# The second product of a dense layer, from the third unit on, as three passes of float16 halves

## Chip, core and metric

One core of one Trainium2 chip runs the whole program. Its engines are TensorE (PE; its weight loads are listed as PEld), VectorE (DVE), ScalarE (ACT), GpSimd (POOL) and SyncE (SP, which here only issues DMAs). The metric is device time in microseconds (us) of one launch, the median of several runs. Shares and durations come from one profiled execution.

## What is computed

Attention with a top-32 mask, then a dense layer with softplus (the "first expert layer"), then a layer of eight routed experts. All inputs are float32 or wider; the tokens are 4 x 576 = 2304, the width is 512.

```python
def _attn_ref(q, k, v):                       # (4, 8, 576, 64)
    scores = scale * np.matmul(q, k.transpose(0, 1, 3, 2))
    kth = np.partition(scores, -top_k, axis=-1)[..., -top_k:-top_k + 1]
    scores = np.where(scores >= kth, scores, -1000000000.0)
    ...
    return np.matmul(attn, v)

def _moe_ref(x, w_in, w_out):                 # 2304x512, 512x2048, 2048x512
    h = x @ w_in
    g = np.maximum(h, 0.0) + np.log1p(np.exp(-np.abs(h)))
    return g @ w_out

def _moe2_ref(x, w_gate, w1, w2):             # 8 experts, 512x1024 and 1024x512
    expert_idx = np.argmax(x @ w_gate, axis=1)
    ...
    out[mask] = gate_w[mask, None] * (np.maximum(xe @ w1[e], 0.0) @ w2[e])
```

## The kernel before

The program has two parts. **Part one** does attention and the dense layer, **part two** the routed experts.

Attention runs over 72 *score groups*, each of two tiles of 128 query rows by 576 keys. A group's scores are made on PE (L406, in two PSUM tiles `sa` and `sb`), copied by ACT (L416, L452), sorted on DVE by eights (L446 to L472) until the 32nd largest is known, masked and exponentiated by ACT and POOL in turn (ACT L480, POOL L481, ACT L482), split into float16 halves (ACT L490, POOL L491 and L492), transposed by DMA (L494) and multiplied with V on PE three groups later (L509, L511, "attention product").

The dense layer runs over ten *units* (`UNITS`, numbered 1 to 10), which become ready as their attention rows are finished. Units 4 and 10 have one tile of 128 tokens, all others two, so 18 tiles in all. A unit takes 16 *steps*, one for each block of 128 of the 2048 hidden columns. In `layer1` a step has 12 float16 matmuls (L596: the split `w_in` against the split `x`), then ACT does Exp (L610, with a sum that is read out) and Ln (L611) and leaves `g`, the block of 128 hidden columns by 256 tokens. Two steps later (`GLAG`) `layer2` multiplies `g` with the block of `w_out` into the PSUM tile `y`, one product of 128x512 for each tile.

For units 1 to 8 that product is a float32 matmul (L636), which the trace shows as two instructions. Units 9 and 10 (`TAIL = 9`) do it in three passes: `g` and the block of `w_out` are each split into two tiles of type float32r by `halves` (ACT copy L622, DVE subtraction L623), and PE takes high by high, high by low and low by high (L633). The tiles for this are borrowed: `g`'s halves sit in the tiles of the pool `raw` in which q, k and v were loaded, `w_out`'s in the tile `w` of the pool `dec`. The block of `w_out` is split again for each of the two units.

`w_out` itself lies as 16 float32 blocks in `w_out_s`, decoded from the input during the first 24 score groups. After a unit's last step its `y` is copied out (L640) and the side steps of `route` follow, one per step, which choose the expert and scatter rows and places to DRAM (SP L702, POOL L705). `early_slots` plans the first slots of part two the same way.

**What sets the order.** Each engine has one queue, executed in order. The program is emitted with priorities (softmax ahead, dense layer behind), and a scheduler then writes each engine's queue; an instruction with free operands may be put far ahead of where it was emitted. Part two's tiles lie in the memory of part one's pools and have to wait until those are free. In part two, `split` (ACT L898, DVE L899) makes float32r halves of expert weights for the products L937 and L950.

## Time and profile before

| | us |
|---|---|
| median of 3 runs (1062.65 to 1066.71) | 1065.49 |
| the profiled execution | 1060.82 |
| its span, first to last instruction | 1059.1 |
| PE busy (share of the span) | 889.8 (84%) |
| DVE busy | 853.0 (81%) |
| ACT busy | 801.3 (76%) |
| POOL busy | 603.0 (57%) |

In the trace, decoding and the first groups fill the first 146 us; units 1 to 8 run beside attention from 147 us on, the last attention product starts at 721 us, units 8 (its end), 9 and 10 fill the time to 822 us, and part two the rest. No engine bounds the whole span: the shares have to be read by stretch. PE's "busy" includes the latency of pipelined matmuls, so its work is better counted as instructions times the distance from one start to the next.

### The profile page before, as it was taken

How to read it: one execution, taken by the hardware profiler on the slowest of the kernel's cores; microseconds unless marked ns; L12 is line 12 of the kernel's file. 1: busy time of each engine (PE TensorE's matmuls, PEld its weight loads, DVE VectorE, ACT ScalarE, POOL GpSimd, SP SyncE). 2: the span in 40 equal slices, each digit the busy share in tenths (PEclk: the TensorE clock that was granted, in tenths of full speed). 3: DMA queues.
4: the chain of work that ended last, by engine and by line, in shares of the span. 5: the costliest groups of instructions: out<-in, count | busy, mean ns of one | idle time of the engine just before them, and what ended most of it. 6: DMA issues, size and time to landing. Idle time of an engine off the chain costs nothing.

```text
span 1059.1 us, 22197 instructions
## 1 busy us (share of the span) xinstructions
PE 889.8 (84%) x7146; PEld 659.0 (62%) x7146; DVE 853.0 (81%) x3021; ACT 801.3 (76%) x1866; POOL 603.0 (57%) x631
## 2 busy tenths in 40 slices
PE   1124379666989797998999999999999999999994
PEld 0012256344656565665666667666787999999993
DVE  5789999899988688997889999965357987777774
ACT  5889899888799678897998898863677655555553
POOL 3889898998678587776877877762001022111111
PEclk9986579777999989998999999999999999999998
DMA  7897898985889987659876755564301667766760
GB/s 189 202 216 165 201 202 176 200 173 100 129 117 171 124 131 136 108 85 150 156 155 113 116 85 98 80 93 124 112 11 32 164 214 240 246 221 220 234 213 24
DMA packets 295859, 156.97 MB, mean 148 GB/s; under 512 B 257524, under 2 KB 257652, under 8 KB 295732
## 3 DMA queue, kind: packets, MB, share of 16 engines
q1 hardware_dynamic: 292116, 145.73, 65.2%
q0 software_dynamic: 3616, 9.72, 2.6%
q8 instruction: 58, 0.95, 0.4%
q14 instruction: 69, 0.57, 0.2%
HBM read 77.89 MB, written 11.11 MB: 84 GB/s over the span
## 4 chain that ended last, share of the span: by engine, by line
PE 47%; DVE 13%; DMA 9%; ACT 8%; POOL 6%; issue 4%; SPq 1%; POOLq 0%; ACTq 0%; DVEq 0%
PE h L937 10%; PE y L950 9%; PE h L596 9%; PE y L636 8%; DVE mx L472 3%; PE y L633 3%; DVE wk L468 3%; POOL e L481 2%; DMA vn<-in_v_dram 2%; DMA kt<-st 2%; DMA pT<-p 2%; PE m L509 1%; PE sb L406 1%; POOL p L492 1%; ACT e L482 1%
## 5 line engine op out<-in xcount | busy, mean ns | idle before, releaser
L636 PE MATMUL y<-w_out_s,g 128*128 128x512 f32 x480 | 233.7, 610 | 5.3 <-ACT g L611 4.7
L596 PE MATMUL h<-xT,w_in_s 128*128 128x256 f16 (+1 forms) x1920 | 224.5, 267 | 9.1 <-POOL w_in_s L260 3.2
L596 PEld LDWEIGHTS <-w_in_s 128*128 128x128 f16 x1920 | 173.6, 100 | 70.2 <-issue 43.6
L481 POOL TENSOR_TENSOR e<-s,e 128x576 f32<-128x576 f32 x144 | 202.5, 1421 | 16.9 <-ACT e L480 16.5
L472 DVE MAX8 mx<-wk 128x8 f32<-128x128 f32 (+2 forms) x432 | 200.8, 500 | 0.1
L492 POOL TENSOR_TENSOR p<-e,p 128x512 f16<-128x512 f32 x144 | 167.3, 1162 | 0.0
L406 PEld LDWEIGHTS <-q 128*128 128x128 f16 (+1 forms) x640 | 56.1, 109 | 175.5 <-issue 127.6
L468 DVE MATCH_REPLACE8 wk<-mx,wk 128x128 f32<-128x128 f32 (+1 forms) x432 | 144.6, 341 | 0.1
L636 PEld LDWEIGHTS y<-w_out_s,g 128*128 128x128 f32 x480 | 83.7, 195 | 69.0 <-issue 57.6
L917 POOL DMA_INDIRECT out_dram<-ot,idx x19 | 19.5, 1028 | 175.7 <-DVE ot L916 172.9
L482 ACT ACTIVATE e<-e,bias 128x576 f32<-128x576 f32 x144 | 110.5, 768 | 11.0 <-POOL e L481 10.4
L406 PE MATMUL sa<-kt,q 128*128 128x256 f16 (+1 forms) x320 | 53.0, 305 | 77.0 <-DMA kt<-st 22.9
L937 PEld LDWEIGHTS h<-xT,wf 128*128 128x128 f32 x864 | 111.8, 191 | 5.3 <-ACT wf L898 0.2
L937 PE MATMUL h<-xT,wf 128*128 128x256 f32 x864 | 113.9, 283 | 0.0
L950 PE MATMUL y<-wf,hT 128*128 128x512 f32 x432 | 112.8, 398 | 0.0
L406 PE MATMUL sb<-kt,q 128*128 128x320 f16 (+1 forms) x320 | 63.1, 340 | 50.9 <-ACT s L452 50.8
L480 ACT ACTIVATE e<-s,kths 128x576 f32<-128x576 f32 x144 | 105.0, 766 | 0.9
L509 PEld LDWEIGHTS <-pT 128*128 128x128 f16 (+1 forms) x1440 | 88.2, 107 | 24.4 <-issue 18.3
L509 PE MATMUL m<-v,pT 128*128 128x65 f16 (+1 forms) x1440 | 95.2, 202 | 9.5 <-DVE x L536 4.9
L490 ACT ACTIVATE p<-e 128x576 f16<-128x576 f32 x144 | 97.4, 678 | 5.0 <-DMA pT<-p 4.3
L491 POOL TENSOR_TENSOR p<-e,p 128x64 f16<-128x64 f32 x144 | 46.1, 320 | 73.6 <-ACT p L490 72.2
L610 ACT ACTIVATE sa<-h 128x256 f32<-128x256 f32 (+1 forms) x160 | 56.3, 352 | 40.1 <-PE h L596 39.3
(213 smaller groups left out, 1817.1 us busy)
## 6 DMA issues: line engine op xcount, KB each, us to landing
w1r<-in_moe_w_dram SPq DMA_DIRECT2D x20, 1024.0 KB
w2r<-in_moe_w_dram SPq DMA_DIRECT2D x20, 1024.0 KB, 6.6
w<-in_moe_w_in_dram SPq DMA_DIRECT2D x16, 512.0 KB, 4.2
w<-in_moe_w_out_dram SPq DMA_DIRECT2D x16, 512.0 KB
rows<-xr SPq DMA_DIRECT2D x37, 128.2 KB, 2.7
qn<-in_q_dram SPq DMA_DIRECT2D x16, 288.0 KB, 3.6
kn<-in_k_dram SPq DMA_DIRECT2D x16, 288.0 KB, 3.1
vn<-in_v_dram SPq DMA_DIRECT2D x16, 288.0 KB, 4.7
```

Of the source, the lines that this page charges most:

```text
L406: last_qk[0] = nc.tensor.matmul(ps[p0:p1], lhsT=qs[:, h, r0:r1, :].rearrange("p r d -> p (r d)"), rhs=kt[:, k0:k1, cs], start=first, stop= ...
L468: nc.vector.match_replace(out=to, in_to_replace=mx[:, i, 8 * j:8 * j + 8], in_values=src[i], imm_value=NEG)
L472: nc.vector.max(out=mx[:, i, 8 * j + 8:8 * j + 16], in_=src[i])
L480: nc.scalar.activation(e[i], s[i], AF.Relu, bias=kths[:, 2 * gi + i], scale=-K_UP)
L481: nc.gpsimd.tensor_tensor(out=e[i], in0=s[i], in1=e[i], op=ALU.subtract)
L482: nc.scalar.activation(e[i], e[i], AF.Exp, bias=bt[:, i], scale=SCORE)
L492: nc.gpsimd.tensor_tensor(out=p16[:, S + D:], in0=e[i][:, 0:S - D], in1=p16[:, 0:S - D], op=ALU.subtract)
L509: nc.tensor.matmul(o[:, h, 0:D + 1], lhsT=pT(r), rhs=v16[:, h, c, 0:D + 1], start=r == 0, stop=r == R - 1)
L596: nc.tensor.matmul(hps[:, :n], lhsT=w_in_s[:, c, j, p, o:o + 128], rhs=xT[:, 0:len(u.tiles), r, c, :], start=m == 0, stop=m == 3 * KD - 1)
L636: nc.tensor.matmul(u.y[i], lhsT=g[:, cs], rhs=w_out_s[:, f, :], start=f == 0, stop=f == KF - 1)
L937: nc.tensor.matmul(h, lhsT=w1f[:, a, c, :], rhs=xT[:, b, c, :], start=n == 0, stop=n == 3 * KD - 1)
L950: nc.tensor.matmul(y[i], lhsT=hT[g][:, a, i * 128:i * 128 + 128], rhs=w2f[:, b, :], start=g == 0 and n == 0, stop=g == KF2 - 1 and n == 2)
```

## The change

From unit 3 on (`HALF_Y = 3` takes the place of `TAIL`) the product is done in three passes of **float16** halves. `w_out` is turned into halves once, while unit 3 runs, and in place: `w_out_t` has one block more at its front, and the two float16 halves of block f are written over float32 block f-1. `g`'s halves are one float16 tile of the size of the old `g`; Ln now writes into Exp's tile `sa`. The subtraction in `halves` moves from DVE to POOL. A sum of the absolute high halves (`y_sums`, 16 ACT instructions emitted with unit 8) goes into the test at the end. The tile `gt` of the softmax goes; its values are kept in a slice of `wk`. Units 1 and 2 stay as they were.

```diff
-TAIL = 9
+HALF_Y = 3
...
+    y_sums = const.tile([128, KF], F32, name="y_sums")
...
-                          (e_sums, 0.0, E_MAX), (w_sums.rearrange("p a b -> p (a b)"), 64.0, 6.0e4)):
+                          (e_sums, 0.0, E_MAX), (w_sums.rearrange("p a b -> p (a b)"), 64.0, 6.0e4),
+                          (y_sums, 64.0, 6.0e4)):
...
-    w_out_s = wp.tile([128, KF, DM], F32, name="w_out_s")
+    w_out_t = wp.tile([128, KF + 1, DM], F32, name="w_out_s")
+    w_out_s = w_out_t[:, 1:]
...
-            gh = row.tile([128, 2, QS], F32, name="gt", bufs=1)
             w2 = row.tile([128, 2, S], F32, name="wk", bufs=WKB)
+            gh = w2[:, :, QS:PS]
...
-            nc.vector.tensor_tensor(out=w2[:, :, QS:PS], in0=gl, in1=gh, op=ALU.min)
+            nc.vector.tensor_tensor(out=gh, in0=gl, in1=gh, op=ALU.min)
...
-        g = gp.tile([128, 256], F32, name="g")[:, :n]
+        half_y = flags is not None and u.number >= HALF_Y
+        g = a[:, :n] if half_y else gp.tile([128, 256], F32, name="g")[:, :n]
...
-        if u.number >= TAIL:
-
-            g2 = raw.tile([128, R * D], F32R, name="qkv"[f % 3] + "n")[:, :2 * n].rearrange("p (s t) -> p s t", s=2)
-            halves(g2, g)
-            w2 = dec.tile([128, 2 * C], F32R, name="w", bufs=DWB).rearrange("p (s c) -> p s c", s=2)
-            halves(w2, w_out_s[:, f, :])
-            g = g2, w2
+            if u.number >= HALF_Y:
+                if u.number == HALF_Y:
+                    halves(w_half(f), w_out_s[:, f, :])
+                g2 = gp.tile([128, 256], F32, name="g").bitcast(F16).rearrange("p (s t) -> p s t", s=2)[:, :, :n]
+                halves(g2, g)
+                g = g2
+            if u.number == len(UNITS) - 2:
+                t = dec.tile([128, C], F32, name="t")
+                nc.scalar.activation(t, w_half(f)[:, 0], AF.Abs, accum_out=y_sums[:, f:f + 1])
...
+    def w_half(f):
+        return w_out_t[:, f, :].bitcast(F16).rearrange("p (s c) -> p s c", s=2)
...
-        nc.vector.tensor_tensor(out=t[:, 1], in0=src, in1=t[:, 0].bitcast(F32), op=ALU.subtract)
+        nc.gpsimd.tensor_tensor(out=t[:, 1], in0=src, in1=t[:, 0], op=ALU.subtract)
...
-            if u.number >= TAIL:
+            if flags is not None and u.number >= HALF_Y:
                 for m, (a, b) in enumerate(PASSES):
-                    nc.tensor.matmul(u.y[i], lhsT=g[0][:, a, cs], rhs=g[1][:, b, :], start=f == 0 and m == 0,
+                    nc.tensor.matmul(u.y[i], lhsT=g[:, a, cs], rhs=w_half(f)[:, b, :], start=f == 0 and m == 0,
                                      stop=f == KF - 1 and m == 2)
```

The line numbers of the changed kernel are higher by 3 to 9 (L406 becomes L409, L596 L599, L610 L614, L636 L645, L633 L642, L898 L907, L937 L946).

**The queues.** The scheduler writes all of them anew. First ACT, at the 27th score group, while unit 2 runs. `s` are copied scores, `e` and `p` the softmax, `sa`, `g` the dense layer's Exp and Ln, `x2T` and `ex` belong to `route`. Before:

```order
L416 ACTIVATE s<-sa 128x2x256
L610 ACTIVATE sa,e_sums<-h 128x256
L490 ACTIVATE p_3538<-e 128x576
L611 ACTIVATE g<-sa 128x256
L479 ACTIVATE kths<-mx 128x2
L480 ACTIVATE e<-s,kths 128x576 x2
L610 ACTIVATE sa,e_sums<-h 128x256
L452 ACTIVATE s<-sb 128x2x320
L611 ACTIVATE g<-sa 128x256
L458 ACTIVATE bias<-mx 128x2
```

The same place in the changed kernel:

```order
L419 ACTIVATE s<-sa 128x2x256
L615 ACTIVATE g<-sa 128x256
L482 ACTIVATE kths<-mx 128x2
L493 ACTIVATE p_3514<-e 128x576
L631 ACTIVATE w_out_s<-w_out_s 128x512
L675 ACTIVATE x2T<-h 128x512
L483 ACTIVATE e<-s,kths 128x576 x2
L624 ACTIVATE t,y_sums<-w_out_s 128x512
L614 ACTIVATE sa,e_sums<-h 128x256
L455 ACTIVATE s<-sb 128x2x320
L461 ACTIVATE bias<-mx 128x2
L631 ACTIVATE w_out_s<-w_out_s 128x512
```

The copies of `w_out` (L631) and the sums emitted with unit 8 (L624) stand here, between the softmax's instructions, with their subtractions in POOL's queue. Counted over the rows of groups 24 to 31: ACT gets 14 copies of `w_out`, 13 sums, 18 Exp where 14 were and 20 Ln or copies of `g` where 14 were; POOL gets 14 subtractions of `w_out` and 4 of `g`. Groups 53 to 61: ACT 20 copies of `g`, 20 Exp for 17, 19 Ln for 17; POOL 21 subtractions of `g`. Groups 62 to 69: 16 copies and 16 subtractions.

PE, from the last attention product on. Before:

```order
L509 MATMUL m<-v_8275,pT 128x65
L690 MATMUL h<-oh,before 128x8
L691 MATMUL h<-ohcum,ones 128x8
L596 LDWEIGHTS w_in_s
L596 MATMUL h<-xT,w_in_s 128x256
...
L636 MATMUL y<-w_out_s,g 128x512 x4
```

In the changed kernel:

```order
L512 MATMUL m<-v_8493,pT 128x65
L599 LDWEIGHTS w_in_s
L599 MATMUL h<-xT,w_in_s 128x256
...
L642 LDWEIGHTS g
L642 MATMUL y<-w_out_s,g 128x512
```

What moved is the place of the last attention product in PE's queue: of the 1920 matmuls of `layer1`, 1464 stood ahead of it before and 1557 now. Behind it, up to part two's first L950, stood 264 `layer1` matmuls of 256 columns, 192 of 128, 16 float32 products and 144 float32r passes; now 171, 192 and 150 float16 passes. The 60 matmuls of part two's L937 that precede the first L950 stood behind unit 10 and are now strewn over units 9 and 10, since ACT's first `split` stands after step 131 of 160 instead of after all of them.

POOL, after the last softmax instruction. `xh` are halves of the dense layer's input, `si` small constants. Before:

```order
L557 TENSOR_TENSOR xh<-xtail_6877,xh 128x512
L1013 IOTA si 128x12
L1013 IOTA si 128x8
L705 DMA table<-ids,dsti 18688x1
L557 TENSOR_TENSOR xh<-x_10337,xh 128x512
L885 DMA xg_12344<-rows,idx 128x513
L885 DMA xg_12346<-rows,idx 128x513
L885 DMA xg_12379<-rows,idx 128x513
L885 DMA xg_12381<-rows,idx 128x513
L705 DMA table<-ids,dsti 18688x1 x5
```

In the changed kernel:

```order
L632 TENSOR_TENSOR g<-sa,g 128x256 x3
L1022 IOTA si 128x12
L1022 IOTA si 128x8
L894 DMA xg_12753<-rows,idx 128x513
L894 DMA xg_12755<-rows,idx 128x513
L560 TENSOR_TENSOR xh<-x_10684,xh 128x512
L632 TENSOR_TENSOR g<-sa,g 128x256 x6
L894 DMA xg_12788<-rows,idx 128x513
L894 DMA xg_12790<-rows,idx 128x513
L632 TENSOR_TENSOR g<-sa,g 128x256 x9
L714 DMA table<-ids,dsti 18688x1
```

POOL's queue was nearly free of compute there; now a subtraction of each step (L632) stands in it behind gathers and scatters.

## Rows read from the trace of the kernel before

**Rows 1.** Stretches: us, busy of PE, PEld, DVE, ACT, POOL, PEclk, DMA, GB/s.
```profile
100.00:200.00 100.00, 67.25 (x559) 43.18 (x558) 96.64 (x303) 91.04 (x203) 89.84 (x86) 0.76 0.86 189
...
264.00:336.00 72.00, 68.62 (x582) 46.12 (x580) 63.21 (x266) 61.53 (x152) 53.65 (x57) 0.98 0.86 136
336.00:538.00 202.00, 183.56 (x1653) 123.72 (x1652) 168.07 (x698) 166.75 (x420) 147.52 (x157) 0.94 0.80 131
538.00:613.00 75.00, 74.15 (x647) 51.11 (x647) 71.69 (x297) 66.75 (x163) 58.97 (x64) 1.00 0.69 116
613.00:678.00 65.00, 64.67 (x590) 44.24 (x587) 63.65 (x265) 57.59 (x136) 49.21 (x53) 1.00 0.58 91
...
722.00:830.00 108.00, 106.47 (x785) 82.86 (x783) 63.30 (x261) 71.82 (x214) 9.90 (x10) 1.00 0.24 69
```

**Rows 2.** First and last start of L509, then of L950, by line.
```profile
L509 PE MATMUL m<-v,pT x1440: 190/193/263, 61.7 to 721.0; 128*128 128x65 f16 x143, 128*64 128x65 f16 x37
...
L950 PE MATMUL y<-wf,hT x432: 387/393/486, 830.4 to 1034.9; 128*128 128x512 f32 x144
```

**Rows 3.** Chain that ended last, in order of time: start, us, what.
```profile
743.10 1.31 PE h L596 x12
744.41 1.72 PE y L636 x4
...
758.98 1.40 PE y L633 x6
...
789.06 0.69 PE h L596 x12
...
797.56 2.99 DMA rows<-xr
...
800.65 0.60 ACT xr L640
```

**Rows 4.** The chain's shares by line, 264 to 336 us, then 336 to 538.
```profile
by line: PE y L636 17.5%; DMA pT<-p 15.7%; PE h L596 11.5%; DMA kt<-st 10.2%; PE sb L406 3.7%; issue 3.6%; PE m L509 3.1%; DVE wk L468 2.7%; DVE mx L472 2.7%; ACT p L490 2.5%; ACT sa L610 2.2%; ACT e L480 2.0%; POOL e L481 2.0%; DVE wk L451
...
by line: PE y L636 15.4%; PE h L596 11.5%; DMA vn<-in_v_dram 7.3%; issue 5.5%; POOL e L481 4.2%; DVE mx L472 3.9%; DMA xT<-xh 3.8%; DMA q<-st 3.6%; DVE wk L468 3.2%; PE sb L406 3.1%; PE m L509 2.7%; DMA kt<-st 2.7%; PE sa L406 2.1%; ACT e L
```

**Rows 5.** Groups by form: line, engine, operation xcount | busy us, mean ns | idle.
```profile
L610 ACT ACTIVATE sa<-h 128x256 f32<-128x256 f32 x128 | 47.7, 373 | 34.2 <-PE h L596 34.0
L610 ACT ACTIVATION_READ_ACCUMULATOR sa<-h 128x1 f32 x160 | 31.5, 197 | 0.0
L611 ACT ACTIVATE g<-sa 128x256 f32<-128x256 f32 x128 | 52.6, 413 | 1.3
L622 ACT ACTIVATE w<-w_out_s 128x512 fp32r<-128x512 f32 x32 | 19.9, 625 | 3.8 <-PE y L633 3.6
L622 ACT ACTIVATE qn<-g 128x256 fp32r<-128x256 f32 x6 | 2.5, 417 | 0.2
L623 DVE TENSOR_TENSOR qn<-g,qn 128x256 fp32r<-128x256 f32 x6 | 2.5, 425 | 11.3 <-ACT qn L622 11.3
L491 POOL TENSOR_TENSOR p<-e,p 128x64 f16<-128x64 f32 x144 | 46.1, 320 | 73.6 <-ACT p L490 72.2 <-issue 0.9
L260 POOL TENSOR_TENSOR w_in_s<-t,w_in_s 128x512 f16<-128x512 f32 x16 | 18.5, 1156 | 2.9 <-ACT w_in_s L259 2.1 <-ACT kths L479 0.8
```

**Rows 6.** Timeline of ACT and of POOL: start, us, what [idle before <-releaser].
```profile
803.54 0.63 ACT L622 ACTIVATE w<-w_out_s 128x512 fp32r<-128x512 f32 x1
804.08 0.29 ACT L622 ACTIVATE kn<-g 128x128 fp32r<-128x128 f32 x1
...
748.83 0.94 POOL L885 DMA_INDIRECT xg<-rows,idx  x1 [12.18 <-DMA idx<-table]
```

**Rows 7.** Timeline of DVE: groups 24 and 32 begin.
```profile
263.55 0.43 DVE L446 TENSOR_TENSOR sb<-sb,s 128x256 f32<-128x256 f32 x1
...
336.00 0.42 DVE L446 TENSOR_TENSOR sb<-sb,s 128x256 f32<-128x256 f32 x1
```

More of the change, by code (lines that the diff above doesn't have):

```diff
@@ L181, in run @@
             late = part_one(tc, p, q, k, v, w_in, w_out, const, ident, before, ones, iota_e, reg_e, wg, ids,
-                            ohcum, done, early, table, rows, flags if halves else None, sums, w_sums, e_sums, kths)
+                            ohcum, done, early, table, rows, flags if halves else None, sums, w_sums, y_sums, e_sums, kths)
         args = w1, w2, out, ident, ones, ohcum, done, early, late, table, rows, meta, left, rare
@@ L201, in part_one @@
 def part_one(tc, ctx, q, k, v, w_in, w_out, const, ident, before, ones, iota_e, reg_e, wg, ids,
-             ohcum, done, early, table, rows, flags, sums, w_sums, e_sums, kths):
+             ohcum, done, early, table, rows, flags, sums, w_sums, y_sums, e_sums, kths):
     nc = tc.nc
```

## The prediction, made before the changed kernel ran

> **What bounds the kernel now.** I read the stretches first, then the chain of waits, then the single instructions. The busy times by stretch show three regimes [rows 1]. From 538 to 678 us, where units 6 and 7 run beside attention, DVE is busy 71.7 of 75 and 63.7 of 65 us: the sorting sets the pace, at 96% and 98%. From 264 to 538 us no engine is full (ACT 61.5 of 72 and 166.8 of 202, DVE 63.2 and 168.1); the chain there is a mixture of PE's matmuls and DMA transposes and loads [rows 4]. From the last attention product at 721.0 us to part two's first L950 at 830.4 us [rows 2] PE is busy 106.5 of 108 us, with ACT at 72 and POOL at 10: a stretch bound by PE alone. A step of unit 8 there is 12 matmuls of 256 columns in 1.31 us and two float32 products in 1.72 us; a step of unit 9 needs 1.40 us for its six float32r passes; 12 matmuls of 128 columns take 0.69 us [rows 3]. Part two behind it keeps its work.
>
> So the change touches two different things: it takes work from PE, which is worth its full price only in the last stretch, and it gives work to ACT and POOL during attention, where they have little room.
>
> **The tail, part by part.** The order says what stands between the last attention product and the first L950. `layer1`: 264 matmuls of 256 columns become 171, since 93 of them (7.75 steps) now stand ahead of that point; 93 x 0.109 (1.31/12) = 10.1 us less. `layer2`: 16 float32 products at 0.86 (1.72/2) and 144 float32r passes at 0.233 (1.40/6) are 13.8 + 33.6 = 47.4 us; they become 150 float16 passes of 512 columns. No row shows such a pass. From above it is bounded by the float32r pass of the same width, 0.233, from below by two float16 matmuls of 256 columns, 0.218, which is the same type; I take 0.218, so 32.7 us. Together 24.8 us less, or 22.5 with the upper price. The 60 matmuls of part two's L937 stand inside this stretch in both kernels; only their place changes, and with it they can fill holes. One hole shows: ACT waits with the copy of `y` until a row DMA is through (2.99 us) and goes on at 800.65 [rows 3]. Of this, and of ACT's copies of `w_out` in unit 10 (0.625 us for each step [rows 5], against a PE step of 0.69 + 0.70), I take 1 us as filled, 0 to 4 as the bounds. The gain in the tail is thus **26 us**.
>
> What can take from it stands in POOL's queue. The product now needs POOL's subtraction, and the subtractions of units 8 to 10 stand behind gathers. Before, POOL waited 12.18 us for the indices of the second pair of gathers [rows 6], with nothing behind it. Now six subtractions stand between the first and the second pair, some 16 us of PE's steps, which covers 12.18; without that cover it would be up to 10 us. I take nothing and keep 10 for the range, so the tail is worth 13 to 29 us.
>
> **Attention, part by part.** Ahead of the last attention product PE has 160 float32 products less (137.6 us), 522 float16 passes more (113.8) and 93 `layer1` matmuls more (10.1): 13.7 us less, but PE is not what ends last there, except in part.
>
> ACT's and POOL's prices: the copy of a `w_out` block 0.625 us, a copy of `g` 0.417, a sum 0.625 + 0.197 for its read-out, Exp 0.373 + 0.197, Ln 0.413 [rows 5]; ACT's instructions overlap, a 0.63 us copy being followed 0.54 us later [rows 6], so I take off 0.09 for each. A subtraction on POOL of 512 columns costs 1.156 us, of 64 columns 0.320 [rows 5]; the straight line between gives 0.68 for 256. Groups 24 and 32 begin at 263.55 and 336.00 us [rows 7], and I take the added instructions of each stretch from the counts of the order.
> - 264 to 336 us: ACT gets 14 copies (8.8), 13 sums (10.7), 4 Exp (2.3) and 6 Ln or copies (2.5), 24.3 us in 54 instructions, less 4.9: 61.5 + 19.4 = 80.9 us in a stretch that took 72 [rows 1]. POOL gets 14 x 1.156 + 4 x 0.68 = 18.9: 72.6. ACT becomes the bound. The fullest that an engine was over such a stretch is DVE's 96.6 of 100 us [rows 1]; at that share it takes 83.7 us, 11.7 more. At least it takes 8.9 more; at ACT's own best, 91.0 of 100, 16.9 more.
> - 538 to 613 us: ACT 20 copies, 3 Exp, 2 Ln, 10.9 us in 28 instructions, so 66.8 + 8.4 = 75.2 of 75; POOL 59.0 + 21 x 0.68 = 73.3. At 96.6% 2.8 us more; bounds 0.2 and 7.6.
> - 613 to 678 us: ACT 57.6 + 6.6 = 64.2 of 65, POOL 49.2 + 10.9 = 60.1; 1.5 us more, bounds 0 and 5.5. DVE, at 98%, is late next: PE's relief buys nothing here.
> - 336 to 538 us: 46 copies (16 of them of 128 columns) bring ACT to about 180 of 202 us, POOL to 175: room, no price. PE's float32 products are 15.4% of the chain there [rows 4], 31 us; at 0.654 for 0.86 they could give back 7.5. With DVE, ACT and DMA close behind I take half, 3.5, bounds 0 and 7.5.
>
> Sum for attention: 11.7 + 2.8 + 1.5 - 3.5 = **12.5 us** more, bounds 1.5 and 30.
>
> The rest: the softmax writes the same five DVE results with `gt` in another place, no instruction more or less, so nothing. The test at the end gets four small DVE instructions in part two, under PE. In place, block f's copy must wait for the subtraction of block f-1 and for unit 2's product f-1; the order has them one step apart, and ACT's price above contains no wait for that.
>
> On the price of POOL the trace shows 256 columns in 0.425 us on DVE (L623) and, by the line above, 0.68 on POOL [rows 5]. The Trainium skill, GPSIMD Engine Reference, section Engine selection, says that a two-input elementwise operation is about twice as slow on GpSimd as on VectorE and belongs on the latter: a rule against this part of the change. By it a subtraction would be 0.85 us, POOL would get 3.6 us more from 538 to 613 us and would be over-full there with 76.9 of 75; the trace agrees in direction, with 1.6 in place of 2.
>
> **Against the measured time.** The profiled execution took 1060.82 us, its span 1059.1, 4.7 us under the median of 1065.49. The sum, -26 + 12.5 = -13.5, gives 1047.3 for a run like that one and 1052.0 against the median.
>
> **The rivals.**
> - *The tail's gain is eaten in attention.* For it: ACT has 80.9 us of work in 72, POOL 72.6, both in order and each waiting for the other. At ACT's best share the cost is 30, and 30 - 26 gives 1069.5. Against it: 336 to 538 us has room. It is no change that can be told (0.5%, about what a measurement of this kernel tells from none, is 5.3 us) when attention costs between 20.7 and 31.3 us.
> - *PE waits for POOL* (slower). Mechanism: `layer2` needs POOL's subtraction, POOL is full at 264 to 336 and 538 to 613 us, and PE's queue has the scores behind that product, so DVE starves. Place: the 98 steps of units 3 to 9 ahead of the last attention product. Price: if one step in five waits for one POOL instruction of 1.16 us, 22.7 us on top of the 12.5: 1074.7. It decides from 18.8 us on, 0.19 us for each step. Against it: two steps lie between a step's Exp and its product, and units 6 and 7 make 32 steps in the 140 us from 538 to 678, 4.4 us each.
> - *Attention hides nearly all of it*: the low bounds, 1.5 and 29, give 1038. For it: the copies of `w_out` may run in ACT's 10.5 idle us from 264 to 336.
> - *A cheaper pass.* The Trainium skill, TensorE: Matmul & The Clock Gate, section Back-to-back issue gap, gives 131 ns for a sustained matmul of 512 columns. The rows have 233 ns for float32r and 109 for 256 columns, so they do not bear it out. As a mechanism of this kernel, a pass at 0.131 would take 150 x 0.087 = 13 us more from the tail: 1039.
> - That the change does not do what it says is excluded by the order, in which 672 float16 passes stand.
>
> **How the numbers follow.** The forecast, faster with both effects near the values taken (1042 to 1060): 0.50. Larger gain by the low bounds: 0.09, by the cheaper pass: 0.01. Eaten, within 5.3 us: 0.23. Slower by PE's wait for POOL: 0.17. Hence faster 0.60, same 0.23, slower 0.17. Faster and eaten alone hold 0.83; the range takes the low bound, 1038, and reaches to 1072, which leaves out the worse half of the slower case.
>
> **What the profile of the changed kernel should show.** The last attention product later than 721.0 us by about 12, most of it between groups 24 and 32, with ACT over 95% busy there; from it to the first L950 some 83 us in place of 109.4, with six float16 passes in 1.31 us; no step of units 8 to 10 waiting on POOL. I am wrong if the passes are no cheaper than float32r's, if PE's idle time before L642 is put down to POOL's L632, or if group 32 starts no later than before.

## The result, and the profile after

The changed kernel is slower: a median of **1075.41 us** (1074.77 to 1078.22) against 1065.16 on the same chip, ratio 1.0094, 95% interval 1.0065 to 1.0124. The profiled execution took 1074.8 us, its span 1073.0, that is 13.9 more than the span of before.

The stretches below begin and end with the same score groups as [rows 1] (group 24, 32, 53, 62, 70), then comes the tail from the last attention product to part two's first product, L959 in this kernel. Columns as in [rows 1].

```profile
267.00:349.50 82.50, 77.26 (x639) 51.68 (x637) 65.26 (x263) 78.13 (x203) 68.56 (x70) 0.98 0.72 118
349.50:556.20 206.70, 170.38 (x1724) 119.03 (x1724) 172.19 (x702) 178.96 (x470) 172.27 (x203) 0.93 0.77 126
556.20:638.50 82.30, 75.67 (x748) 55.87 (x748) 74.85 (x304) 77.30 (x197) 73.39 (x86) 0.98 0.64 116
638.50:706.70 68.20, 66.42 (x674) 46.88 (x673) 64.97 (x275) 62.93 (x160) 58.94 (x69) 1.00 0.56 88
754.50:841.40 86.90, 82.75 (x677) 61.14 (x673) 28.01 (x127) 50.90 (x163) 26.67 (x42) 0.97 0.35 102
```

The tail shrank from 109.4 to 86.9 us, nearly as forecast. The last attention product comes at 754.5 us instead of 721.0: attention is 33.5 us longer, not 12.5. From 349.5 to 556.2 no engine is full (ACT is busy for 179 of 206.7 us), and the stretch is still longer than its counterpart of before.

The chain in the tail shows the steps that the prediction sized:

```profile
778.46 1.31 PE h L599 x12
779.77 1.29 PE y L642 x6
```

Six float16 passes of 512 columns take 1.29 us, 0.215 each, against 1.40 for six float32r passes [rows 3]. The Trainium skill, TensorE: Matmul & The Clock Gate, section Back-to-back issue gap, gives 131 ns for such a matmul in a sustained stream of weight loads and matmuls, and about 216 ns for an isolated one; this trace, where each pass has its weight load, agrees with the second figure and not with the first.

At the tail's end stands something that the prediction did not have. PE's rows, first of the kernel before, then of the changed one (start, us, line, in brackets the idle time before it):

```profile
820.98 0.66 PE L664 MATMUL h<-ident,xr 128*128 128x128 f32 x4 [0.69 <-ACT xr L640]
821.50 3.41 PE L937 MATMUL h<-xT,wf 128*128 128x256 f32 x24
824.75 0.95 PE L670 MATMUL h<-wg,x2T 128*128 128x8 f32 x8
825.58 4.58 PE L937 MATMUL h<-xT,wf 128*128 128x256 f32 x36
830.36 4.34 PE L950 MATMUL y<-wf,hT 128*128 128x512 f32 x18
...
835.09 0.66 PE L673 MATMUL h<-ident,xr 128*128 128x128 f32 x4 [0.69 <-ACT xr L649]
836.43 1.88 PE L679 MATMUL h<-wg,x2T 128*128 128x8 f32 x8 [0.69 <-ACT x2T L675]
839.60 0.57 PE L699 MATMUL h<-oh,before 128*128 128x8 f32 x2 [1.28 <-DVE oh L696]
840.02 0.57 PE L700 MATMUL h<-ohcum,ones 128*128 128x8 f32 x2
841.47 6.71 PE L959 MATMUL y<-wf,hT 128*128 128x512 f32 x18 [0.88 <-DVE ohcum L706]
```

Before, the routing of unit 10 ran under 60 products of part two (24 in 3.41 us and 36 in 4.58). In the changed kernel those 60 (L946) had gone ahead, most of them between 790 and 820 us, and the routing stands bare: seven steps that wait for each other, from 834 to 841.5. The granted clock falls within it, from the higher of its two levels (2.4 GHz, 1.00) to the lower one (1.2 GHz, 0.50), and stays there for the first products of part two; it is the third column from the right:

```profile
831.40:836.20 4.80, 3.29 (x24) 1.53 (x22) 3.04 (x17) 2.24 (x7) 1.85 (x3) 1.00 0.14 30
836.20:846.40 10.20, 7.80 (x24) 6.59 (x25) 3.15 (x17) 1.48 (x5) 0.99 (x1) 0.50 0.13 28
846.40:851.40 5.00, 5.00 (x30) 4.41 (x29) 3.98 (x20) 2.31 (x5) 0.00 (x0) 0.99 0.32 7
```

The eight products of the routing at 836.43 take 1.88 us, against 0.95 before. Part two's first 18 products, most of them at the lower clock, take 6.71 us, against 4.34 for the same 18 before: 2.4 us, which is most of the 2.6 by which part two is longer (207.1 against 204.5 from the first to the last product).

### The profile page after: what moved, and what is told of

Its sections match the earlier page's. It is cut to its first block, busy times and chain, and to the rows that moved or that the text cites. A ratio compares the mean times of both kernels' runs of the same rounds, so it can differ in the third digit from the quotient of the medians.

```text
span 1073.0 us, 22946 instructions
## 1 busy us (share of the span) xinstructions
PE 863.7 (80%) x7322; PEld 644.8 (60%) x7322; DVE 838.8 (78%) x2961; ACT 825.3 (77%) x1978; POOL 692.8 (65%) x775
## 4 chain that ended last, share of the span: by engine, by line
PE 43%; DVE 14%; DMA 13%; POOL 11%; issue 7%; ACT 7%; SPq 3%; POOLq 0%; ACTq 0%; DVEq 0%
PE h L946 10%; PE y L959 10%; PE h L599 8%; PE y L642 6%; DVE mx L475 3%; POOL e L484 3%; DMA pT<-p 3%; DVE wk L471 3%; POOL p L495 2%; DMA q<-st 2%; DMA v<-vs 2%; PE sb L409 2%; DMA w<-in_moe_w_in_dram 2%; PE m L512 1%; PE y L645 1%
## 5 line engine op out<-in xcount | busy, mean ns | idle before, releaser
L599 PE MATMUL h<-xT,w_in_s 128*128 128x256 f16 (+1 forms) x1920 | 224.7, 269 | 21.4 <-ACT w_in_s L262 5.8
L599 PEld LDWEIGHTS <-w_in_s 128*128 128x128 f16 x1920 | 177.0, 101 | 69.3 <-issue 24.0
L484 POOL TENSOR_TENSOR e<-s,e 128x576 f32<-128x576 f32 x144 | 202.2, 1417 | 9.0 <-ACT e L483 8.5
L642 PE MATMUL y<-w_out_s,g 128*128 128x512 f16 x672 | 176.9, 387 | 10.1 <-ACT g L631 6.4
L409 PEld LDWEIGHTS <-q 128*128 128x128 f16 (+1 forms) x640 | 57.6, 109 | 188.4 <-issue 145.8
L409 PE MATMUL sb<-kt,q 128*128 128x320 f16 (+1 forms) x320 | 64.2, 344 | 75.6 <-ACT s L455 75.4
L946 PEld LDWEIGHTS h<-xT,wf 128*128 128x128 f32 x864 | 112.8, 191 | 5.8
L946 PE MATMUL h<-xT,wf 128*128 128x256 f32 x864 | 116.0, 285 | 0.0
L959 PE MATMUL y<-wf,hT 128*128 128x512 f32 x432 | 115.2, 405 | 0.9 <-DVE ohcum L706 0.9
L632 POOL TENSOR_TENSOR g<-sa,g 128x256 f16<-128x256 f32 (+1 forms) x128 | 78.1, 614 | 56.2 <-ACT g L631 44.3
L512 PE MATMUL m<-v,pT 128*128 128x65 f16 (+1 forms) x1440 | 98.8, 206 | 14.8 <-DVE x L539 6.0
L512 PEld LDWEIGHTS <-pT 128*128 128x128 f16 (+1 forms) x1440 | 91.0, 109 | 28.4 <-issue 22.8
L409 PE MATMUL sa<-kt,q 128*128 128x256 f16 (+1 forms) x320 | 53.4, 307 | 63.8 <-DMA kt<-st 24.2
L642 PEld LDWEIGHTS <-g 128*128 128x128 f16 x672 | 62.7, 101 | 64.3 <-ACT g L631 10.1
L959 PEld LDWEIGHTS y<-wf,hT 128*128 128x128 f32 x432 | 78.5, 193 | 14.6 <-DVE ohcum L706 1.0
```

Source lines behind the costliest of these rows:

```text
L409: last_qk[0] = nc.tensor.matmul(ps[p0:p1], lhsT=qs[:, h, r0:r1, :].rearrange("p r d -> p (r d)"), rhs=kt[:, k0:k1, cs], start=first, stop= ...
L484: nc.gpsimd.tensor_tensor(out=e[i], in0=s[i], in1=e[i], op=ALU.subtract)
L512: nc.tensor.matmul(o[:, h, 0:D + 1], lhsT=pT(r), rhs=v16[:, h, c, 0:D + 1], start=r == 0, stop=r == R - 1)
L599: nc.tensor.matmul(hps[:, :n], lhsT=w_in_s[:, c, j, p, o:o + 128], rhs=xT[:, 0:len(u.tiles), r, c, :], start=m == 0, stop=m == 3 * KD - 1)
L642: nc.tensor.matmul(u.y[i], lhsT=g[:, a, cs], rhs=w_half(f)[:, b, :], start=f == 0 and m == 0, stop=f == KF - 1 and m == 2)
L946: nc.tensor.matmul(h, lhsT=w1f[:, a, c, :], rhs=xT[:, b, c, :], start=n == 0, stop=n == 3 * KD - 1)
```

## The experiments

One table first, since the verdicts rest on it. Each row is a profiled execution, cut where group 24, 32, 53, 62 and 70 begin (first maximum of the group on VectorE), at the last attention product, and at part two's first product; "part two" runs to the last of those products. The ratio is that to the kernel before, run on the same chip; half the width of its interval is 0.003 to 0.007. A median of one chip is not to be set against one of another: use the ratios for that. That single executions differ by a few us shows in e13, whose time is that of before (0.9995): its last attention product comes at 726.2 us, 5.2 later than in the profiled run of before, which lay 4.7 us under its median.

| kernel | to 24 | 24-32 | 32-53 | 53-62 | 62-70 | 70-last | tail | part two | median | ratio |
|---|---|---|---|---|---|---|---|---|---|---|
| before | 263.6 | 72.4 | 201.9 | 74.9 | 65.3 | 42.9 | 109.4 | 204.5 | 1065.2 | 1 |
| after | 267.0 | 82.5 | 206.7 | 82.3 | 68.2 | 47.8 | 86.9 | 207.1 | 1075.4 | 1.0094 |
| e1 halves from unit 9 | 264.7 | 78.9 | 195.7 | 81.3 | 66.7 | 49.1 | 115.2 | 206.7 | 1085.5 | 1.0229 |
| e2 halves from unit 8 | 266.6 | 77.3 | 195.8 | 81.2 | 75.4 | 45.5 | 100.0 | 206.8 | 1074.7 | 1.0117 |
| e3 no subtraction of g | 266.4 | 84.0 | 217.4 | 77.1 | 65.5 | 48.4 | 94.6 | 206.4 | 1086.4 | 1.0228 |
| e4 no sums | 267.5 | 80.5 | 212.4 | 83.4 | 67.6 | 47.1 | 84.6 | 207.2 | 1078.1 | 1.0153 |
| e5 before without gt | 269.1 | 73.8 | 200.0 | 84.6 | 66.1 | 44.5 | 111.5 | 206.4 | 1077.5 | 1.0121 |
| e6 after with gt | 261.9 | 83.0 | 202.4 | 82.8 | 68.7 | 46.5 | 86.6 | 206.5 | 1070.4 | 1.0055 |
| e7 e6, from unit 8 | 262.4 | 75.7 | 203.2 | 84.8 | 72.7 | 53.3 | 93.1 | 207.3 | 1078.6 | 1.0142 |
| e8 e6, from unit 9 | 263.6 | 77.5 | 203.1 | 84.0 | 65.4 | 49.0 | 108.3 | 207.4 | 1082.2 | 1.0168 |
| e9 before, swap | 265.2 | 79.6 | 203.8 | 79.1 | 65.5 | 43.0 | 111.2 | 204.6 | 1077.7 | 1.0133 |
| e10 before, swap 2 | 267.2 | 72.8 | 198.1 | 80.5 | 65.4 | 51.6 | 104.0 | 204.5 | 1071.4 | 1.0067 |
| e11 after, swap | 266.3 | 83.8 | 214.1 | 86.9 | 68.1 | 47.8 | 90.1 | 207.2 | 1090.9 | 1.0248 |
| e12 e6, swap | 264.3 | 87.4 | 203.2 | 83.8 | 68.4 | 50.3 | 84.4 | 206.6 | 1074.8 | 1.0103 |
| e13 before, swap, same queues | 265.3 | 72.9 | 203.6 | 77.0 | 65.0 | 42.5 | 109.5 | 204.5 | 1064.4 | 0.9995 |
| e14 e5, swap | 265.1 | 77.1 | 202.2 | 79.3 | 67.1 | 48.5 | 104.2 | 204.6 | 1071.7 | 1.0051 |
| e15 e6, from unit 4 | 264.1 | 75.7 | 213.9 | 81.2 | 67.8 | 47.6 | 87.4 | 206.8 | 1071.1 | 1.0068 |
| e16 e6, w_out on VectorE | 263.8 | 86.3 | 210.6 | 90.1 | 66.4 | 47.0 | 87.4 | 206.0 | 1080.9 | 1.0136 |
| e17 e6, sums late | 266.4 | 78.6 | 200.0 | 86.0 | 69.9 | 49.8 | 88.7 | 207.4 | 1071.9 | 1.0125 |
| e18 e17, from unit 5 | 264.3 | 75.0 | 221.5 | 83.5 | 67.1 | 49.5 | 83.2 | 207.6 | 1080.7 | 1.0203 |

**The added work, taken away piece by piece.** The first theory was that the added instructions of units 3 to 9 cost what attention lost; the rivals named POOL's subtractions of g and ScalarE's sums.

```diff
-HALF_Y = 3
+HALF_Y = 9        (e1; the sums with unit 9.  e2: HALF_Y = 8)
```

> HALF_Y = 9: only units 9 and 10 use float16 halves; w_out is split in place while unit 9 runs, the sums go with unit 9. If attention's extra work is what cost the time, attention is as before (last attention product at 721 us, give or take 5) and the tail keeps a small gain (float16 for float32r passes, no second split of w_out in unit 10, part two begun earlier): 4 to 8 us under the kernel before, about 1059. If the new arrangement of the queues itself is to blame (another layout of the pools), it is no faster than before: 1065 to 1072.

> HALF_Y = 8: units 8 to 10, all of whose steps but a few lie behind the last attention product. By the order 216 layer1 matmuls of 256 columns stand in the tail (264 before), no float32 product (16) and 169 float16 passes (144 float32r): 16 us less of PE there, 3 us more in attention: about 1051. If the tail's price per pass were wrong, it would not be faster than 1060.

```diff
-                halves(g2, g)
+                nc.scalar.activation(g2[:, 0], g, AF.Copy)       (e3)
...
-                    ... lhsT=g[:, a, cs], rhs=w_half(f)[:, b, :] ...
+                    ... lhsT=g[:, 0, cs], rhs=w_half(f)[:, b, :] ...
```

> The changed kernel without the subtraction of g's halves on POOL: the third pass takes the high half of g a second time, so g's low half is left out; ACT's copies, the split of w_out and three passes stay. POOL theory (the subtractions in POOL's full queue delay the softmax and the product): attention falls by 15 to 20 us, the time to 1055 to 1060. ACT theory (copies and sums): 0 to 4 us less, 1071 to 1075.

```diff
-            if u.number == len(UNITS) - 2:
-                t = dec.tile([128, C], F32, name="t")
-                nc.scalar.activation(t, w_half(f)[:, 0], AF.Abs, accum_out=y_sums[:, f:f + 1])
+    nc.vector.memset(y_sums, 1024.0)                             (e4)
```

> The changed kernel without the 16 sums of absolute halves (y_sums is set once; the test then always passes for it). ACT theory: 13 of them stood between groups 24 and 32, where ACT had 80.9 us of work for 72; 8 to 10 us less there, the time 1066. POOL theory: 0 to 3 us less, 1072 to 1075, since POOL's 14 subtractions of w_out still stand there.

None of the four gave attention back all that it had lost. With halves only from unit 9 on, attention up to group 70 holds the same work as before (but for one of the 16 blocks of `w_out`, halved early), yet the last attention product comes 15.4 us later (736.4), and with a longer tail (115.2) the time is 2.3% longer. Without POOL's subtraction of g (the third pass takes the high half of g again) the kernel is slower than with it, without the sums no faster. So a part of the loss is not the added work.

**The tile gt.** The edit that all these share is the softmax tile `gt`, which the prediction had priced at nothing.

```diff
-            gh = row.tile([128, 2, QS], F32, name="gt", bufs=1)
+            gh = w2[:, :, QS:PS]                                 (e5: this alone, in the kernel before)
```

e6 gives the tile back to the changed kernel; the halves of block 0 of `w_out` then lie in a tile of the pool `dec`. e7 and e8 are e6 with `HALF_Y = 8` and `9`.

> The kernel before with one part of the change alone: the tile gt is removed, its contents go into the middle slice of wk, as in the changed kernel; everything else (float32 products, three-pass tail) stays. Theory A (the lost tile costs attention time: L447 has to wait until wk, with its single buffer, is free of the group before it, so VectorE's five operations of a new group no longer fit between the selections of the old one): slower than before by 8 to 25 us, group 18 begins some 8 us later, the last attention product comes at 730 to 745 us instead of 721, PE's wait in front of the sb tile grows from 50.8 us towards 75. Theory B (tile placement is worth nothing; the loss comes from the float16 halves and the earlier start of the second part): within 0.5% of before, last attention product 719 to 723.

> The changed kernel with the tile gt given back; the spare block for w_out's halves moves to a free buffer of the decoding pool instead, so the float16 halves and all passes stay as they are. Theory A: attention wins back most of the 21 us by which it missed the prediction, last attention product 730 to 740 instead of 754.5, the time 1050 to 1062. Theory B: last attention product 750 to 758, the time 1072 to 1080.

> As the run before, but with halves from unit 8 on only. Theory A: with the tile back and the added work of units 3 to 7 gone, attention stands within 5 us of before (last attention product 721 to 726), the tail at some 98 us instead of 109.4: 1050 to 1058. Theory B: as with halves from unit 8 and no tile, 1073 to 1078.

> As the run before, but with halves from unit 9 on only, so attention up to group 72 has no added work at all, and the tile gt is there as in the kernel before. Theory A: attention as before (last attention product 719 to 724), the tail near that of before: 1060 to 1068. Theory B: last attention product 733 to 739 as in the run with halves from unit 9 and no tile, 1080 to 1088.

e5 was as slow as the theory said, and e6 a little faster than the changed kernel. e7 pays for its halving of `w_out`, which stands in unit 8, from group 62 on. But e8, which has the tile and no added work ahead of group 70, lost more than e1: 742.6 for the last attention product. Of its 21.6 us, 6.8 lie between the starts of groups 59 and 60. The chain of waits there, then ScalarE's row:

```profile
594.94 0.44 POOL table L716
595.38 9.59 DMA xT<-xh
605.00 0.63 ACT xh L559
605.62 0.37 ACT sa L614 x2
...
605.00 0.63 ACT L559 ACTIVATE xh<-x 128x512 f16<-128x512 f32 x1 [5.09 <-DMA xT<-xh]
```

A transpose `xT` was issued at 595.38 and landed 9.59 us later; ScalarE's next copy into `xh` (a single buffer) waited 5.09 us for it, with an Exp of the dense layer and a copy of scores behind it in the queue. That points to where an instruction stands in a queue, rather than to how much work there is.

**The order alone.** So the next theory (D) was that the queues of before are a good draw among the orders that the scheduler may write. It was tried with edits that hold no work at all: two neighbouring independent operations written in the other order.

```diff
-            nc.vector.tensor_tensor(out=w2[:, :, :QS], in0=gl, in1=gh, op=ALU.max)
             nc.vector.tensor_tensor(out=w2[:, :, QS:PS], in0=gl, in1=gh, op=ALU.min)
+            nc.vector.tensor_tensor(out=w2[:, :, :QS], in0=gl, in1=gh, op=ALU.max)     (e9; e12 in e6)
```

```diff
-            nc.vector.tensor_copy(w2[:, :, PS:PS + US], ps[:, :, PS:PS + US])
             nc.vector.tensor_tensor(out=w2[:, :, PS + US:], in0=ps[:, :, :PS], in1=s2[:, :, :PS], op=ALU.min)
+            nc.vector.tensor_copy(w2[:, :, PS:PS + US], ps[:, :, PS:PS + US])          (e10)
```

```diff
-            nc.vector.tensor_tensor(out=gl, in0=ps[:, :, :QS], in1=s2[:, :, :QS], op=ALU.max)
             nc.vector.tensor_tensor(out=gh, in0=ps[:, :, QS:PS], in1=s2[:, :, QS:PS], op=ALU.max)
+            nc.vector.tensor_tensor(out=gl, in0=ps[:, :, :QS], in1=s2[:, :, :QS], op=ALU.max)  (e13; e11 in after, e14 in e5)
```

> The kernel before with two neighbouring VectorE operations of the softmax written in the other order (L448 and L449, a maximum and a minimum of the same two operands into two slices of wk). No work is added or taken away. The scheduler nevertheless writes other queues: 12 of the 160 Exp of the dense layer move past a score group on ScalarE, 139 of 912 DMAs move past a transpose pT on SP. Theory D (much of what was lost in attention is the order: the queues of before are an unusually good draw, and any edit that makes the scheduler write them anew costs some 10 us, in single stalls of ScalarE or PE behind late DMAs): slower by 6 to 18 us, and the stretch from group 53 to group 62 grows from 74.9 us to 80 or more, as in nearly every variant so far. Theory A (the loss comes from the work and the tiles that the change moves): within 3 us of before.

> The kernel before with another neutral swap: L450 (a copy) and L451 (a minimum), which write different slices of wk. 27 of 160 Exp and 117 of 912 DMAs move past a group. Theory D: again slower by 6 to 18 us, at other places than the first swap. Theory A: within 3 us of before.

> The changed kernel with a neutral swap (its first two maxima, into gl and gh, in the other order). 38 of 160 Exp and 142 of 912 DMAs move past a group. Theory D: the changed kernel is already an ordinary draw, so it moves by up to 8 us in either direction, 1067 to 1083, and not by the same stretches. Theory A: within 3 us of the changed kernel, 1072 to 1078.

> The changed kernel with the tile gt given back (as e6) and the swap of the maximum and the minimum: 43 of 160 Exp and 113 of 912 DMAs move past a group against e6. Theory D: 1062 to 1078, a draw about e6's 1070. Theory A: within 3 us of e6.

> The kernel before with its first two maxima (L446 and L447) in the other order. This swap leaves ScalarE's, POOL's and SP's queues as they were in attention: 0 of 160 Exp, 0 of 912 DMAs move past a group; on VectorE 26 small operations move. Theory D (the order of the queues that DMAs and ScalarE stand in is what the other swaps paid for): within 3 us of before, and group 53 to 62 within 2 us of 74.9. Rival (the swap of operations itself costs): slower by 6 us or more, as the other two swaps.

> The kernel before without the tile gt (as e5), with its first two maxima in the other order; against e5, 30 of 160 Exp and 142 of 912 DMAs move past a group. Theory A (the missing tile has a price of its own): group 18 again begins 8 to 11 us later than before, and the time is 1072 to 1085. Theory D (e5 was only a bad draw): group 18 anywhere from 199 to 206 us, the time anywhere from 1065 to 1080.

Two swaps of nothing cost 1.33% (13 us) and 0.67% (7 us). The third costs nothing (0.9995, 0.9966 to 1.0024); after it, SP's 1146 instructions and POOL's 631 stand in the trace in the order of before, and ScalarE's 1866 but for one. So the redrawn order is what the first two pay for. An edit that redraws it can be expected to pay some such amount, though two swaps and two edits of gt are few to size it by. e11 shows the largest move: the changed kernel became 1.5% slower through a swap.

One place where e9 lost 5.5 us (start of group 26 to group 27) can be followed. SP's queue of before, then of e9:

```profile
276.75 1.25 SPq L718 DMA_DIRECT2D rows<-xr  x2
279.54 14.91 SPq L494 DMA_TRANSPOSE pT<-p  x4
...
275.53 1.09 SPq L718 DMA_DIRECT2D rows<-xr  x2
276.91 22.27 SPq L494 DMA_TRANSPOSE pT<-p  x5
```

L718 is a fill of rows in DRAM. Of the 144 transposes L494, 46 are issued ahead of it in before and 45 in e9: one now stands behind it instead of ahead. From the list of DMA issues, and from the chains of before and of e9 at that place:

```profile
rows<-xr SPq DMA_DIRECT2D x1, 1154.2 KB
...
279.54 11.32 DMA pT<-p
290.95 0.68 ACT p L490
...
276.91 16.93 DMA pT<-p
293.92 0.16 ACT p L490
```

The first transpose behind the 1154 KB takes 11.32 us to land in before and 16.93 in e9. In before one tile more had got through ahead of the fill; in e9 ScalarE stands at L490 until 293.92 instead of 290.95, and group 28 begins at 305.6 instead of 298.2.

For gt alone this leaves no price that can be told: e5 and e14 (1.0121, 1.0051) lie where e9 and e10 lie (1.0133, 1.0067). A trace of it remains early on: group 18 begins at 207.4 to 210.5 us in the eight kernels without the tile, and at 199.6 to 203.9 with it, but most of that is given back by group 24.

**Where the added work is paid.** What remained was the price of the work itself, above all of halving `w_out`.

```diff
-HALF_Y = 3
+HALF_Y = 4        (e15, in e6)
```

> The changed kernel with gt given back and halves from unit 4 on (HALF_Y = 4): the halving of w_out (16 copies on ScalarE, 16 subtractions on POOL) stands a unit later, where before ScalarE has 64.5 and POOL 59.0 us of work in 83.5. The tail is as with HALF_Y = 3. If the halving is what fills group 24 to 32 (83 us in e6): that stretch falls to 72 to 78 us, group 32 to 53 grows by less than 4 us over e6's 202.4, and the time is 1060 to 1067. If the order alone decides: no such shift between the stretches, 1066 to 1080.

```diff
-                    halves(w_half(f), w_out_s[:, f, :])
+                    t = w_half(f)
+                    nc.scalar.activation(t[:, 0], w_out_s[:, f, :], AF.Copy)
+                    nc.vector.tensor_tensor(out=t[:, 1], in0=w_out_s[:, f, :], in1=t[:, 0], op=ALU.subtract)   (e16, in e6)
```

> As e6 (gt back, halves from unit 3), with the 16 subtractions of w_out's halves on VectorE in place of POOL; g's subtractions stay on POOL. In the changed kernel's chain POOL's w_out subtractions are 10% of the stretch from group 24 to 32, where VectorE has 17 us to spare. If they are the price there: 75 to 80 us for that stretch in place of 83.0, the time 1062 to 1068. If ScalarE's copies and sums are (78.0 of 83.0 us busy): 81 to 85, the time 1067 to 1076.

```diff
-            if u.number == len(UNITS) - 2:
+            if u.number == len(UNITS) - 1:
...
-                nc.scalar.activation(t, w_half(f)[:, 0], AF.Abs, accum_out=y_sums[:, f:f + 1])
+                with tc.issue_after(ex_i.ins):
+                    nc.scalar.activation(t, w_half(f)[:, 0], AF.Abs, accum_out=y_sums[:, f:f + 1])   (e17, in e6; e18 also HALF_Y = 5)
```

> As e6 (gt back, halves from unit 3), with the 16 sums of w_out's high halves written behind the Exp of unit 9 on ScalarE, by an order edge; in e6 the scheduler had put them between groups 20 and 31. 13 sums at 0.73 us are 9.5 us of ScalarE's work less between groups 24 and 32. If added work costs some 0.6 us for each us there: that stretch falls from 83.0 to 75 to 79 us, and the time to 1062 to 1068. If the order alone decides: 81 to 87 us, the time 1066 to 1080. The tail has room for them (ScalarE 51 of 87 us busy) and stays within 2 us of 86.6.

> As the run before, with halves from unit 5 on (HALF_Y = 5): the halving of w_out stands between groups 39 and 47, units 3 and 4 keep float32 products. Work theory: group 24 to 32 within 73 to 79 us, group 32 to 53 at 203 to 210, the last attention product at 738 to 746, the tail at 86 to 88, so 1058 to 1067. Order alone: 1066 to 1080.

Stretches of e15 (24 to 32, 32 to 40), of before (32 to 40), of e17 (24 to 32), of before and of e18 (40 to 53):

```profile
264.10:339.80 75.70, 68.75 (x567) 45.35 (x566) 64.61 (x268) 61.37 (x147) 52.38 (x55) 0.94 0.77 126
339.80:435.10 95.30, 80.99 (x709) 54.73 (x707) 71.54 (x279) 84.70 (x222) 79.11 (x83) 0.96 0.76 124
...
336.00:419.50 83.50, 73.20 (x610) 48.83 (x609) 65.48 (x270) 64.47 (x153) 58.99 (x64) 0.92 0.85 133
...
266.40:345.00 78.60, 70.69 (x595) 46.62 (x594) 62.99 (x266) 68.66 (x167) 68.11 (x70) 0.98 0.75 123
...
419.50:537.90 118.40, 110.33 (x1043) 74.85 (x1042) 102.54 (x429) 102.19 (x266) 88.43 (x94) 0.96 0.76 129
...
420.80:560.80 140.00, 118.77 (x1137) 81.26 (x1134) 110.42 (x440) 120.38 (x313) 118.16 (x129) 0.94 0.67 109
```

e15 shows the halving's price most plainly. Moved by a unit, it leaves the stretch from 24 to 32 at 75.7 us instead of 83.0, and the next one is 95.3 instead of 83.5, though ScalarE is busy for 84.7 of that and POOL for 79.1. The chain of that stretch, by line, points to why: the sums (L624, 5.5% or 5.2 us) and the subtractions of `w_out` (L634, 3.4% or 3.2 us) stand on it between the softmax's own links, and so do five copies (L633) of 0.52 us each.

```profile
by line: DMA q<-st 9.5%; issue 7.7%; POOL e L484 7.1%; ACT t L624 5.5%; ACT e L483 5.3%; ACT p L493 5.0%; DVE oh L698 4.4%; DMA kt<-st 4.1%; PE h L599 3.7%; POOL p L495 3.5%; ACT sa L614 3.5%; POOL w_out_s L634 3.4%; ACT e L485 3.3%; ACT s 
```

In e18 the halving lies between 425 and 512 us, from group 40 to group 48, and group 40 to 53 takes 140.0 us instead of 118.4; its time, too, is longer than both of its forecasts. In e17 only the sums are gone from attention: ScalarE has 68.7 us to do from 24 to 32 instead of 78.0, and the stretch is 78.6 instead of 83.0, inside the forecast; the time did not follow, since other stretches of the redrawn order lost it again (to group 24, and 53 to 62). e16 fell outside its forecast: POOL is relieved (56.3 us busy), the stretch is longer (86.3). So POOL's fullness alone is not the price there. In each of these runs the order is redrawn as well, so that a difference of a few us in one stretch proves little.

None of these versions beats the kernel before. e6 comes nearest (1.0016 to 1.0094).

## Why the prediction was wrong

The sum forecast 13.5 us less than the profiled run of before, whose span would have been 1045.6; it is 1073.0, 27.4 more. In the medians the miss is 23.4, since the profiled run of before was 4.7 us under its median. By steps, of the 27.4:

- **The tail**, forecast −26, measured −22.5, and part two +2.6 where it was to keep its work. The float16 pass was taken at 0.218 and is 0.215. The hole that was to be filled did the opposite: the 60 products of part two which covered unit 10's routing were used up earlier, the routing stands bare (PE is idle for 3.8 us from 832.0 to 841.4, of 4.2 in the whole tail), and the clock falls in it. Together 6.1 us. The prediction had no step of units 8 to 10 waiting on POOL; six weight loads of the tail did, for 2.5 us in all.
- **264 to 336 us**, forecast +11.7, measured +10.1 (82.5 against 72.4). ScalarE is busy for 78.1 of 82.5, 94.7%, near the 96.6% of the step (its sign was over 95%). That it landed there does not prove the rule by which it was sized: by that rule (96.6% of a full engine) e15's 84.7 us of ScalarE need 87.7 us, and took 95.3; e18's 120.4 need 124.6, and took 140.0; e17's 68.7 need less than the 72.4 of before, and took 78.6.
- **336 to 538 us**, "room, no price", forecast −3.5, measured +4.8: 8.3 us, the largest miss of a term in the sum. Its cause stays open. In e6, e12 and e17, which have about the same copies and subtractions of `g` there and the tile gt, the stretch takes 202.4, 203.2 and 200.0 us, no more than in the four kernels whose order was redrawn but which hold none of the added work (e5, e9, e10, e14: 198.1 to 203.8). There the room was room, and only the 3.5 us did not come. In the kernels with added work and without the tile (the changed kernel, e3, e4, e11) it takes 206.7 to 217.4, so the loss of gt, which the prediction priced at nothing, may cost something together with the added work; but e16 has the tile and takes 210.6. What e15 and e18 show is that a halving of `w_out` placed there is not free (+11.8 us in its stretch in e15, +21.6 in e18, there with 19 copies of `g`), although ACT and POOL have idle time: the softmax's chain passes through both of their queues in turn, and an added copy between two links can delay the next link.
- **538 to 613 and 613 to 678 us**, forecast +2.8 and +1.5, measured +7.4 and +2.9. (By its own rule of 0.09 us off for each copy the second has 62.8 us of ACT's work, not 64.2, and no price.) In e5, e9, e10 and e14 the first of these stretches takes 79.1 to 84.6 us. So 82.3 is what a redrawn order gives, not what the work adds.
- **The ends of attention**, not in the sum: up to group 24 +3.4, from group 70 to the last product +4.9. In e5, e9, e10 and e14 these pieces take 265.1 to 269.1 and 43.0 to 51.6 us, so here too the changed kernel (267.0 and 47.8) lies where a redrawn order lies. The chain in front of the last product names part two's early slots on VectorE, which were placed ahead of the last group's end (before, the same instruction starts at 728.1 us, behind the last product), and the last transpose behind them:

```profile
733.24 0.19 DVE x L539
733.50 0.10 DVE flags L478
733.60 4.95 DVE eci L738
...
750.86 3.21 DMA pT<-p
754.12 0.20 PE m L512
```

- **PE waits for POOL**, the slower rival, is not what happened: over the whole span PE's weight loads wait 8.8 us for the subtraction L632, 15 times, far from the 22.7 of that rival. The slower case that did happen had no rival; the nearest is the one whose gain is eaten in attention.

The step that failed most is one that the prediction did not write down: it set its sum against the profile of before as if the queues around the edit stayed as they were, so a redrawn order stood at nothing. The order had shown that many instructions move. Against kernels with a redrawn order the change reads otherwise. Means over e5, e9, e10 and e14 without the added work, and over after, e6, e11 and e12 with it: last attention product 737.3 and 756.1 us, tail 107.7 and 87.0, part two 205.0 and 206.9. So the work costs 18.8 us in attention (the bounds were 1.5 and 30, the value 12.5) and 1.8 in part two, and gives back 20.7 in the tail: about nothing. By stretch, the work costs 8.3 us from group 24 to 32 (forecast 11.7), 5.6 from 32 to 53 (−3.5), 3.1 from 53 to 62 (2.8) and 2.3 from 62 to 70 (1.5): with the order set apart, the second is the term that was far off.

What made the changed kernel slower is then mostly the draw: the mean ratio of the four kernels without the work is 1.0093, 9.9 us, and the changed kernel's is 1.0094. This is argued from means and not shown for this kernel. The four with the work have a mean ratio of 1.0125, so by the ratios the work costs some 3 us more than nothing; their last attention products lie 21.7 us apart (3.6 in the group without the work), so their mean is known to a few us only. The change with all other instructions held in the order of before was not run; it would settle it. Why the scheduler's queues of before suit the chip better than those of its neighbours was followed at two places (the fill L718, the transpose `xT`), not for the whole.

## What to carry to other kernels

Where a scheduler writes the queues, a well-tuned kernel's time belongs partly to its order: write down a term for redrawing it, sized by a few edits without work, before the terms of the edit itself. Idle time of an engine that a dependency chain passes through need not be room: here the stretch with the halving of `w_out` became 10 to 22 us longer for 16 to 20 us of added work on ScalarE, wherever it stood, a redrawn order included. Before filling a hole with work from elsewhere, look at which later hole that work now leaves bare.

## What the runs showed of the hardware

- The first DMA transpose behind a fill of 1154 KB on the same queue landed 11.3 us after its issue in before and 16.9 us after it in e9; elsewhere a transpose took 3.2 us (750.86 in the changed kernel) and another, `xT`, 9.6 us (595.38 in e8), so the fill is not shown to be the only cause. The transpose itself is issued in 1.3 us where it does not wait.
- The granted clock was 1.00 from 831.4 to 836.2 us, where PE was busy for 3.29 of 4.80 us, and 0.50 (the lower level, 1.2 GHz) for the next 10.2 us; 18 products of 512 columns, most of them in that stretch, took 6.71 us against 4.34 before.
- POOL's subtraction of 256 columns to float16 takes 0.674 us, as the straight line between 64 and 512 columns gave (0.68); on VectorE a subtraction of that width, to float32r, took 0.425 [rows 5]. The Trainium skill, GPSIMD Engine Reference, section Engine selection, says about twice as slow; here it is 1.6 times. Moving the subtractions of `w_out` to VectorE (e16) was nevertheless slower than e6 (1.0136 against 1.0055), of which the redrawn order can be a part.
